# Windowed attention with a gated MLP: one free list for PSUM's eight banks, MLP sums read out by halves, a shorter weight decode, and another order of the work

## The chip, the cores and the metric

The kernel runs on one core of a Trainium2 chip. The metric is device time in microseconds (us); before the change the median of three runs is 635.64, from 635.51 to 636.7. The engines are called as the profile calls them: PE (TensorE, matmuls), PEld (its weight loads), DVE (VectorE), ACT (ScalarE), POOL (GpSimd) and SP (SyncE, which issues all DMAs).

## What is computed

Attention over a window of 128 positions with a linear bias per head, and behind it an MLP whose second half is normalised and mixed along the sequence, for 8 batches, 8 heads of 64, 576 positions:

```python
def _attn_ref(q, k, v):
    scores = scale * np.matmul(q, k.transpose(0, 1, 3, 2))
    mask = (rel >= 0) & (rel < 128)
    scores = np.where(mask, scores + bias[None], -1000000000.0)
    attn = np.exp(scores - np.max(scores, axis=-1, keepdims=True))
    attn = attn / (np.sum(attn, axis=-1, keepdims=True) + 1e-09)
    return np.matmul(attn, v)

def _moe_ref(x, w_in, g_ln, w_sg, b_sg, w_out):      # x: 8 x 576 x 512, the heads side by side
    h = gelu_tanh(x @ w_in)                          # 1024 columns
    u, v = h[..., :512], h[..., 512:]
    v_n = (v - mean(v)) / np.sqrt(var(v) + 1e-06) * g_ln
    v_s = np.einsum('ts,bsd->btd', w_sg, v_n) + b_sg[None, :, None]
    return x + (u * v_s) @ w_out
```

`w_in` and `w_out` are float64. They come to the chip as 64-bit words and are decoded there.

## The kernel before

**The attention.** The work is cut into 32 pairs: 8 batches of 4 pairs of heads. For each pair there are steps, each named by a letter and the pair's number: `q` and `L` load queries with keys, and values (SP); `a` and `c`, or `*` for both, compute the scores (PE, L247); `A`, `B`, `C`, `G` select and take row minima of the negated scores (DVE, L273 and L266); `e`, `E`, `f`, `F`, `j` are exponentials with their row sums (ACT, L282), written into a column of `stats`, ten to a pair; `R` adds 1e-9 and inverts (DVE, L294 and L295); `r`, `s`, `S` scale (POOL, L299); `t`, `T`, `z` transpose on PE (L309, L322); `X`, `Y`, `P` mask and copy the transposes (DVE L318, ACT); `2` with `v`, or `3` with `V`, are the sums with the values (PE, L329 and L342); `x` copies the result out of PSUM (ACT, L350 and L351); `h`, `l`, `k` split it into a high and a low part (ACT L356, POOL L359, ACT L362).

**The MLP.** Each product is three matmuls, high by high, high by low and low by high (`mm3`, L555 to L561). For batch b: `v{b}{t}` are the sums of the v half for row block t (in batch 0 in pieces `w{t}{c}`), `vg` their gelu out of PSUM (ACT, L633), `nv…` the steps of the norm; `tt`, `tj`, `tg`, `nt…`, `tn` do the same for the last 64 rows, the tail (tn is L595); `u{b}{f}{i}` are the sums of the u half for feature block f and half i of the 576 positions (288 columns each), `uc` copies a block's two halves into an array (ACT, L689), `ug` is the gelu over all of it; `y{b}{f}{i}` mix v along the positions, `gm` multiplies u by both halves (DVE, L712), `gh` and `gl` split the product (ACT L716, POOL L719); `Oa` and `O` are the output sums, `oa` adds x to both halves (DVE, L742) and `D` stores (SP, L754). PE takes the same number of matmuls of the same widths for all of this wherever in the program they stand.

**The weights.** Each 64-bit weight block k goes through `i` (load, SP L168), `d` (ACT, L179 and L181), `m` (DVE, L183), `b` (DVE, L185), `o` (DVE, L187), `+` (POOL, L190), `H` (ACT, L192) and `-` (L194), twelve blocks, all while the first batch is under way. The buffers `wst` that the loads fill are four, and are later used for g. The mixing weights w_sg are staged through the same buffers (`wl`, `wH`, `w-`, L522 and L523; `gb` loads g_ln).

**PSUM.** PSUM has eight banks of 512 f32 columns. Before, pool `ps_s` has two single banks, `ps_a` two single banks, and `ps_m` two tiles of two banks each. Scores and value sums use `ps_s` or `ps_a`, transposes `ps_a`, and all MLP sums `ps_m`: two row blocks of v share one tile, one bank each, and so do the two halves of a u, y or o sum.

**The order.** Nothing is reordered: the list ORDER (L780 to L841) names every step once, 1684 in all, and each engine runs its instructions in the list's order. A planner (L385 to L408) only holds that a step stands behind what it needs. So an engine whose next instruction waits holds up everything behind it; on SP that holds for a DMA that waits for a free buffer. The loop at the end of the kernel ties each instruction to the one before it on its engine.

Of the kernel before, what the change touches and what calls it, by code (L numbers as in the profile page):

```python
# [9 lines left out]
F32 = mybir.dt.float32  # L10
# [11 lines left out]
def attention_gmlp(  # L22
# [30 lines left out]
    TINY64 = 2.0 ** -15  # L53
# [16 lines left out]
    def hi_of(x):  # L70
        return x[:, 0:S]
# [99 lines left out]
    def split64(hi, lo, w, f, last):  # L171
# [9 lines left out]
        nc.scalar.activation(f, w1f, AF.Abs)  # L181
        yield
        nc.vector.tensor_scalar(f, f, TINY64, None, ALU.max)  # L183
        yield
        nc.vector.tensor_scalar(fi, fi, 3, 0x3FFFFFFF, ALU.logical_shift_left, ALU.bitwise_and)  # L185
        yield
        nc.vector.scalar_tensor_tensor(out=fi, in0=w1, scalar=-0x40000000, in1=fi, op0=ALU.bitwise_and, op1=ALU.bitwise_or)  # L187
# [20 lines left out]
    class Pair:  # L208
# [25 lines left out]
        def scores(self, *t2s):  # L234
            insts = [x for t2 in t2s for x in self.score_list(t2, ps_a if len(t2s) > 1 and t2 == 0 else ps_s)]
            burst(insts)

        def score_list(self, t2, pool):
# [5 lines left out]
            banks = self.banks[t2] = [pool.tile([P, 512], F32, name=pool.name) for _ in range(2)]  # L244
# [47 lines left out]
        def inverse(self):  # L292
            rr = self.rr = att.tile([P, NS], F32, name="rr", bufs=3)
            nc.vector.tensor_scalar(rr, self.sm, 1e-9, None, ALU.add)  # L294
            nc.vector.reciprocal(rr, rr)  # L295
# [11 lines left out]
        def transpose(self, j):  # L307
            ct = self.ct[j] = ps_a.tile([P, 512], F32, name="ps_a")
# [11 lines left out]
        def transpose_first(self):  # L320
            self.ct0 = ps_a.tile([P, 512], F32, name="ps_a")
# [5 lines left out]
        def values_first(self, pool):  # L327
            self.x2 = pool.tile([P, 512], F32, name=pool.name)
            nc.tensor.matmul(self.x2[:, 0:R], self.vd, self.p0, start=True, stop=True)  # L329
# [31 lines left out]
        def low_tail(self):  # L361
# [9 lines left out]
            "T": lambda p: p.transpose(1), "Y": lambda p: p.masked(1), "2": lambda p: p.values_first(ps_a), "v": lambda p: p.values(ps_a), "3": lambda p: p.values_first(ps_s), "V": lambda p: p.values(ps_s), "x": gather, "h": high, "l": low, "k": low_tail,  # L371
# [13 lines left out]
    class Planner:  # L385
# [23 lines left out]

    BUFS = {"ps_s": 2, "ps_a": 2, "ps_m": 2, "e": 4, "qk": 2, "vt": 2, "nb": 3, "rr": 3, "px": 2, "xf": 2 * NC, "xs": NC, "g": NF, "vg": 2, "vn": 1, "vA": 1, "u": 1, "st": 3}  # L410
# [23 lines left out]
    def add_pair(n):  # L434
# [441 lines left out]
```

## Time and profile before

| what | value |
|---|---|
| median of 3 runs | 635.64 us |
| the profiled execution's own time | 635.48 us |
| its span in the trace | 633.8 us |
| instructions in the span | 14834 |
| mean granted clock of PE | 0.985 |
| moved by DMA | 57.24 MB |

The span is what the trace covers, from the first instruction to the last; the time of the same execution is 1.7 us more. In rows of the timeline the columns are the start, the busy time of the group, engine, line, operation, what is written and read, count, and in brackets how long the engine was idle before it and what ended that. In rows that group a line, the numbers are the least, median and greatest duration in ns and the first and last start in us. A row of a stretch gives its ends and length, then the busy time of PE, PEld, DVE, ACT and POOL with the number of instructions, the granted clock of PE as a share of full speed, the busy share of the DMA engines and GB/s.

### The profile page before, as it was taken

How to read it: one execution, taken by the hardware profiler on the slowest of the kernel's cores; microseconds unless marked ns; L12 is line 12 of the kernel's file. 1: busy time of each engine (PE TensorE's matmuls, PEld its weight loads, DVE VectorE, ACT ScalarE, POOL GpSimd, SP SyncE). 2: the span in 40 equal slices, each digit the busy share in tenths (PEclk: the TensorE clock that was granted, in tenths of full speed). 3: DMA queues.
4: the chain of work that ended last, by engine and by line, in shares of the span. 5: the costliest groups of instructions: out<-in, count | busy, mean ns of one | idle time of the engine just before them, and what ended most of it. 6: DMA issues, size and time to landing. Idle time of an engine off the chain costs nothing.

```text
span 633.8 us, 14834 instructions
## 1 busy us (share of the span) xinstructions
PE 603.6 (95%) x5664; PEld 550.9 (87%) x5664; DVE 374.3 (59%) x1297; ACT 355.4 (56%) x1047; POOL 232.7 (37%) x237
## 2 busy tenths in 40 slices
PE   2687999989999999999999999999999999999997
PEld 1466799978999989998899989998999989999896
DVE  4779897537654786455723577647564565462611
ACT  6687768462673854834672578647473455543430
POOL 2668635542135222542134333542235221441220
PEclk9878999999999999999999999999999999999999
DMA  5777503241203243131220432333122311110001
GB/s 211 223 229 236 158 31 116 79 143 38 73 18 97 95 140 93 42 112 41 78 79 2 134 133 78 86 108 97 40 95 79 128 65 41 41 40 38 0 1 76
DMA packets 55931, 57.24 MB, mean 90 GB/s; under 512 B 8498, under 2 KB 45362, under 8 KB 55860
## 3 DMA queue, kind: packets, MB, share of 16 engines
q1 hardware_dynamic: 55860, 56.28, 28.5%
q8 instruction: 45, 0.74, 0.5%
q14 instruction: 26, 0.21, 0.1%
HBM read 46.83 MB, written 9.44 MB: 89 GB/s over the span
## 4 chain that ended last, share of the span: by engine, by line
PE 85%; DVE 4%; ACT 2%; issue 1%; POOL 0%; POOLq 0%; DVEq 0%
PE ps_m L559 21%; PE ps_m L561 20%; PE ps_m L560 20%; PE ps_s L342 8%; PE ps_a L309 4%; PE ps_a L247 4%; PE ps_s L247 3%; ACT e L282 1%; PE ps_m L707 1%; PE ps_m L706 1%; PE ps_m L643 1%; PE ps_m L645 1%; PE ps_s L329 1%; DVE px L318 1%; DVE e L266 1%
## 5 line engine op out<-in xcount | busy, mean ns | idle before, releaser
L282 ACT ACTIVATE e<-e,stats 128x128 f32<-128x128 f32 (+1 forms) x320 | 121.2, 381 | 39.4 <-DVE stats L266 38.4
L299 POOL TENSOR_TENSOR e<-e,rr 128x512 f32<-128x512 f32 (+1 forms) x96 | 80.1, 854 | 134.6 <-DVE rr L295 99.0
L559 PE MATMUL ps_m<-g,wo 128*128 128x288 f32 x256 | 78.7, 308 | 0.0
L559 PE MATMUL ps_m<-ws,vn 128*128 128x288 f32 x256 | 78.6, 307 | 0.0
L559 PE MATMUL ps_m<-xs,wi 128*128 128x288 f32 x256 | 77.6, 303 | 0.1
L561 PE MATMUL ps_m<-g,wo 128*128 128x288 f32 x256 | 75.8, 296 | 0.0
L561 PE MATMUL ps_m<-xs,wi 128*128 128x288 f32 x256 | 75.6, 295 | 0.0
L560 PE MATMUL ps_m<-ws,vn 128*128 128x288 f32 x256 | 75.6, 295 | 0.0
L561 PE MATMUL ps_m<-ws,vn 128*128 128x288 f32 x256 | 75.5, 295 | 0.0
L560 PE MATMUL ps_m<-xs,wi 128*128 128x288 f32 x256 | 75.5, 295 | 0.0
L560 PE MATMUL ps_m<-g,wo 128*128 128x288 f32 x256 | 74.9, 293 | 0.5 <-POOL g L719 0.5
L584 POOL TENSOR_TENSOR rs<-rs,mhalf 128x1 f32<-128x1 f32 (+1 forms) x40 | 31.4, 786 | 109.5 <-DVE rs L581 103.7
L359 POOL TENSOR_TENSOR xs<-xf,xs 128x576 fp32r<-128x576 f32 x32 | 45.4, 1425 | 62.0 <-ACT xs L356 62.0
L318 DVE TENSOR_TENSOR px<-ps_a,m_old 128x512 f32<-128x512 f32 x64 | 43.9, 686 | 41.1 <-PE ps_a L309 27.3
L719 POOL TENSOR_TENSOR g<-u,g 128x576 fp32r<-128x576 f32 x32 | 45.5, 1424 | 51.0 <-ACT g L716 51.0
L282 ACT ACTIVATION_READ_ACCUMULATOR e<-e,stats 128x1 f32 (+1 forms) x320 | 60.3, 188 | 0.0
L247 PE MATMUL ps_s<-qk 64*64 64x192 f32 (+2 forms) x632 | 42.2, 354 | 14.1 <-DMA qk<-qkT 7.9
L559 PE MATMUL ps_m<-wi,xs 128*128 128x512 f32 x128 | 53.6, 419 | 2.1 <-ACT vg L633 2.1
L712 DVE TENSOR_TENSOR u<-ps_m,u 128x576 f32<-128x576 f32 x32 | 24.1, 755 | 52.0 <-PE ps_m L707 49.8
L742 DVE TENSOR_TENSOR xf<-ps_m,xf 128x576 f32<-128x576 f32 x32 | 24.0, 752 | 49.3 <-PE ps_m L561 49.3
L560 PE MATMUL ps_m<-wi,xs 128*128 128x512 f32 x128 | 51.3, 401 | 0.0
L559 PEld LDWEIGHTS ps_m<-xs,wi 128*128 128x128 f32 x256 | 48.3, 188 | 3.4 <-issue 1.6
(122 smaller groups left out, 1523.4 us busy)
## 6 DMA issues: line engine op xcount, KB each, us to landing
qk<-qkT SPq DMA_DIRECT2D x32, 576.0 KB, 3.9
vt<-v_in SPq DMA_DIRECT2D x64, 256.0 KB, 3.5
outT<-xf SPq DMA_DIRECT2D x32, 288.0 KB, 2.1
wst<-w_in SPq DMA_DIRECT2D x8, 512.0 KB, 6.1
vt<-v_in SPq DMA_DIRECT2D x64, 32.0 KB, 3.1
wst<-w_out SPq DMA_DIRECT2D x4, 512.0 KB, 3.9
wst<-w_sgT SPq DMA_DIRECT2D x4, 288.0 KB, 5.1
vd<-v_in SPq DMA_DIRECT2D x64, 16.0 KB, 2.7
```

The source lines that it names most:

```text
L247: return lambda: nc.tensor.matmul(dst, qk[js, 0, q0:q0 + R], qk[js, 1, k0:k1], start=True, stop=True)
L282: nc.scalar.activation(x, x, AF.Exp, bias=self.nm[0:n, i:i + 1], scale=-1.0, accum_out=self.sm[0:n, i:i + 1])
L299: nc.gpsimd.tensor_tensor(x, x, self.rr[0:n, i:i + m].rearrange("p (m o) -> p m o", o=1).broadcast_to([n, m, c]), ALU.mult)
L309: burst([lambda t=t: nc.tensor.transpose(ct[:, t * P:(t + 1) * P], self.pr[j][:, t, :], ident) for t in range(T)])
L318: nc.vector.tensor_tensor(xv[:, :, :, i, :], cv, m.rearrange("p (t h c) -> p t h c", t=1, h=1).broadcast_to([P, T, 2, R]), ALU.mult)
L342: return lambda: nc.tensor.matmul(x1[heads[j], q0 + lo // 2 * R if t < 0 else q0 + t * R:q0 + (hi + 1) // 2 * R], block, px[j][:, (half * ...
L359: nc.gpsimd.tensor_tensor(lo_of(self.xs), self.xf, hi_of(self.xs).bitcast(F32), ALU.subtract)
L559: nc.tensor.matmul(dst, ah, bh, start=(first and i == 0), stop=False)
L560: nc.tensor.matmul(dst, ah, bl, start=False, stop=False)
L561: nc.tensor.matmul(dst, al, bh, start=False, stop=(last and i == n - 1))
L584: nc.gpsimd.tensor_tensor(x["rs"][0:rows], x["rs"][0:rows], mhalf[0:rows], ALU.pow)
L719: nc.gpsimd.tensor_tensor(st[f"g{f}"][:, 1, :], st["u"][:, f, :], st[f"g{f}"][:, 0, :].bitcast(F32), ALU.subtract)
```

## The change

Five edits.

1. **Decode.** Step `m`, the maximum with TINY64, is gone for all twelve blocks. ACT's Abs (L181) multiplies by a constant REBASE, the shift has no mask behind it, and the combine takes only the sign bit.
2. **PSUM.** The three pools become eight fixed one-bank tiles. The planner hands them out while it goes through the order: a step gets the bank that has been free longest, and a bank is free again when the last step that reads it stands in the order ahead of the new one. Any step can get any bank.
3. **Halves.** Each v, u, y and o sum has a bank of its own, and what reads a sum reads one half: two copies `uc`, two multiplications `gm` and two additions `oa` of 288 columns each in place of one of 576. `Oa` and `O` are split the same way; `D` waits for both halves.
4. **Eleven columns.** `stats` and `rr` have one column more, so that L294 and L295 run over eleven columns in place of ten.
5. **The order.** ORDER is a new list, of 1808 steps.

```diff
-    TINY64 = 2.0 ** -15
+    REBASE = 2.0 ** (-(1023 - 127) // 8)
...
-    ps_s = ctx.enter_context(tc.tile_pool(name="ps_s", bufs=2, space=PSUM))
-    ps_a = ctx.enter_context(tc.tile_pool(name="ps_a", bufs=2, space=PSUM))
-    ps_m = ctx.enter_context(tc.tile_pool(name="ps_m", bufs=2, space=PSUM))
+    ps = ctx.enter_context(tc.tile_pool(name="ps", bufs=1, space=PSUM))
+    NB = 8
+    psum = [ps.tile([P, 512], F32, name=f"bank{i}") for i in range(NB)]
+    given = []
+
+    def bank():
+        return psum[given.pop(0)]
...
-        x = const.tile([P, 2, NS], F32, name=f"stats{i}")
+        x = const.tile([P, 2, NS + 1], F32, name=f"stats{i}")
...
-        nc.scalar.activation(f, w1f, AF.Abs)
+        nc.scalar.activation(f, w1f, AF.Abs, scale=REBASE)
         yield
-        nc.vector.tensor_scalar(f, f, TINY64, None, ALU.max)
+        nc.vector.tensor_scalar(fi, fi, 3, None, ALU.logical_shift_left)
         yield
-        nc.vector.tensor_scalar(fi, fi, 3, 0x3FFFFFFF, ALU.logical_shift_left, ALU.bitwise_and)
-        yield
-        nc.vector.scalar_tensor_tensor(out=fi, in0=w1, scalar=-0x40000000, in1=fi, op0=ALU.bitwise_and, op1=ALU.bitwise_or)
+        nc.vector.scalar_tensor_tensor(out=fi, in0=w1, scalar=-0x80000000, in1=fi, op0=ALU.bitwise_and, op1=ALU.bitwise_or)
...
-            rr = self.rr = att.tile([P, NS], F32, name="rr", bufs=3)
+            rr = self.rr = att.tile([P, NS + 1], F32, name="rr", bufs=3)
...
+            at = {n: i for i, n in enumerate(order)}
+            free = [-1] * NB
             for n in order:
                 _, _, _, run, after, _, take, _, _ = self.steps[n]
                 assert done.issuperset(after), n
                 for c, users in take:
+                    if c == "ps":
+
+                        i = free.index(min(free))
+                        assert free[i] < at[n], n
+                        free[i] = max(at[u] for u in users)
+                        given.append(i)
+                        continue
...
             def run():
-                key = f"pv{t // 2 * 2}"
+                key = f"pv{t}"
                 if key not in st:
-                    st[key] = ps_m.tile([P, 2, 512], F32, name="ps_m")
+                    st[key] = bank()
...
-            def gate():
-                u = st["u"][:, f, :]
-                nc.vector.tensor_tensor(in2(u), st[f"py{f}"][:, :, 0:S2], in2(u), ALU.mult)
+            def gate(i):
+                def run():
+                    u = st["u"][:, f, halves[i]]
+                    nc.vector.tensor_tensor(u, st[f"py{f}{i}"][:, 0:S2], u, ALU.mult)
+                return run
...
-        y731 Oa7 gm73 gh73 gl73 O70 O72 oa70 D70 O73 oa72 D72 O71 oa73 D73 oa71 D71
+        gl71 gl70 gl72 Oa71 Oa70 gm730 oa631 D63 gh73 gl73 O700 O701 oa700 oa701 O730 oa730 oa600 O731 oa731 O720 O721 oa720
+        oa721 D72 D62 D73 D60 D70 D61 O710 O711 oa710 oa711 D71
```

Three places where the order moves instructions. In the changed kernel line numbers differ a little: L168 has become L172, L185 L187, L187 L189, L273 L275, L266 L268, and `mm3`'s L559 to L561 are L569 to L571.

The first is the start of SP's list, which issues all loads. `wst` are the decode buffers (weights), `qk` queries with keys of one pair, `vt` and `vd` the values of one pair. Before:

```order
L168 DMA wst<-w_in 128x512
L221 DMA qk<-qkT 128x1152
L168 DMA wst<-w_sgT 128x576
L221 DMA qk<-qkT 128x1152
L168 DMA wst<-w_in 128x512 x2
L168 DMA wst<-w_sgT 128x576 x2
L550 DMA gb<-g_ln 128x512
L221 DMA qk<-qkT 128x1152
L168 DMA wst<-w_in 128x512
L229 DMA vt<-v_in 128x4x128
```

The changed kernel's start of the same list:

```order
L223 DMA qk<-qkT 128x1152
L172 DMA wst<-w_in 128x512 x3
L223 DMA qk<-qkT 128x1152
L172 DMA wst<-w_in 128x512
L223 DMA qk<-qkT 128x1152
L231 DMA vt<-v_in 128x4x128
L232 DMA vt<-v_in 64x128
L231 DMA vt<-v_in 128x4x128
```

Pair 0's queries have become the first load; its values stand behind four weight blocks, the number of the buffers, and the mixing weights behind those values.

The second place is DVE's start: the decode of the first two or three weight blocks (`tmp`) among pair 0's minima (the select into PSUM; each is followed by its minima, left out here). Before, it goes on from the second half of pair 0's first scores:

```order
L183 TENSOR_SCALAR tmp<-tmp 128x512 x2
L185 TENSOR_SCALAR tmp<-tmp 128x512
L187 SCALAR_TENSOR_TENSOR tmp<-wst,tmp 128x512
L185 TENSOR_SCALAR tmp<-tmp 128x512
L273 COPY_PREDICATED ps_s<-sel,ps_s 128x2x64
```

The changed kernel, from the same half on:

```order
L275 COPY_PREDICATED bank_68<-sel,bank_68 128x2x64
...
L187 TENSOR_SCALAR tmp<-tmp 128x512
L189 SCALAR_TENSOR_TENSOR tmp<-wst,tmp 128x512
L275 COPY_PREDICATED bank_69<-sel,bank_69 128x2x64
...
L275 COPY_PREDICATED bank_70<-sel,bank_70 128x2x64
```

Before, five decode steps of two weight blocks stand between the two halves of the minima of pair 0. In the changed kernel the shift of the second block and the first block's combine are left there, and the shift of a third block comes behind pair 0's last minima.

The third place is PE at the first two v sums of batch 1, v10 and v11 (`xs` the split attention result, `wi` the weights, `g` and `wo` those of the output sums). Before, the end of v10 and the start of v11:

```order
L561 MATMUL ps_m_1777<-wi_141,xs_1612 128x512
L559 MATMUL ps_m_1777<-wi_141,xs_1658 128x512 [waits Activation_49]
L560 MATMUL ps_m_1777<-wi_141,xs_1658 128x512
L561 MATMUL ps_m_1777<-wi_141,xs_1658 128x512 [waits Pool_49]
L559 MATMUL ps_m_1777<-wi_141,xs_1649 128x512 [waits Activation_49]
L560 MATMUL ps_m_1777<-wi_141,xs_1649 128x512
```

The changed kernel, the end of v11 and the start of v10:

```order
L571 MATMUL bank1_68<-wi_143,xs_1604 128x512 [waits Pool_49]
L569 MATMUL bank5_72<-g_1377,wo_144 128x288 [waits DVE_49]
...
L570 MATMUL bank5_72<-g_1379,wo_144 128x288
L571 MATMUL bank5_72<-g_1379,wo_144 128x288
L569 MATMUL bank6_73<-wi_143,xs_1527 128x512 [waits DVE_49]
```

Both sums had the same tile, and the second waited for ACT at its first matmul; now they have two banks with twelve matmuls of an output sum between them, and the second waits for a DVE step there.

More of the change, by code (lines that the diff above doesn't have):

```diff
@@ L234, in scores, with score_list @@
         def scores(self, *t2s):
-            insts = [x for t2 in t2s for x in self.score_list(t2, ps_a if len(t2s) > 1 and t2 == 0 else ps_s)]
+            insts = [x for t2 in t2s for x in self.score_list(t2)]
             burst(insts)
-        def score_list(self, t2, pool):
+        def score_list(self, t2):
             qk, heads = self.qk, self.heads
@@ L243, in score_list @@
                 self.e0 = e0s[self.n % 2]
-            banks = self.banks[t2] = [pool.tile([P, 512], F32, name=pool.name) for _ in range(2)]
+            banks = self.banks[t2] = [bank() for _ in range(2)]
             def score(dst, js, q0, k0, k1):
@@ L307, in transpose @@
         def transpose(self, j):
-            ct = self.ct[j] = ps_a.tile([P, 512], F32, name="ps_a")
+            ct = self.ct[j] = bank()
             burst([lambda t=t: nc.tensor.transpose(ct[:, t * P:(t + 1) * P], self.pr[j][:, t, :], ident) for t in range(T)])
@@ L320, in transpose_first @@
         def transpose_first(self):
-            self.ct0 = ps_a.tile([P, 512], F32, name="ps_a")
+            self.ct0 = bank()
             nc.tensor.transpose(self.ct0[:, 0:P], self.e0, ident)
@@ L452, in add_pair @@
         else:
-            put("*", "PE", 1.9, [f"q{n}", ("z", n - 2)], take=es + [("ps_a", [f"A{n}"]), ("ps_a", [f"B{n}"]), ("ps_s", [f"C{n}"]), ("ps_s", [f"G{n}"])])
+            put("*", "PE", 1.9, [f"q{n}", ("z", n - 2)], take=es + [("ps", [f"A{n}"]), ("ps", [f"B{n}"]), ("ps", [f"C{n}"]), ("ps", [f"G{n}"])])
             put("A", "DVE", 0.9, [f"*{n}", ("R", n - 3)])
@@ L654, in his @@
                 return [st["vA"][0:R], vB[0:R]]
-            add(f"tt{b}", "PE", 1.9, at, sums, [f"k{n}" for n in mine] + rows + [f"{k}{c}" for c in range(NC) for k in "-H"], take=[("ps_m", [f"tj{b}"])])
+            add(f"tt{b}", "PE", 1.9, at, sums, [f"k{n}" for n in mine] + rows + [f"{k}{c}" for c in range(NC) for k in "-H"], take=[("ps", [f"tj{b}"])])
             add(f"tj{b}", "DVE", 1.35, at - AHEAD, join, [f"tt{b}"], take=[("vg", [f"tn{b}"]), ("vg", [f"tj{b}"])])
@@ L722, in add_y @@
                 need = [f"tn{b}", f"nt{b}h"] + [f"vn{b}{t}" for t in range(T)] + (["t-", "b-", "tH"] + [f"w-{c}" for c in range(T)] if b == 0 else [])
-                add(f"y{b}{f}{i}", "PE", 1.87, at + 1.87 * STRETCH * i, sums(i), need + ([f"y{b}{f}0"] if i else []), take=[] if i else [("ps_m", [f"gm{b}{f}"])])
-            add(f"gm{b}{f}", "DVE", 0.69, at - AHEAD, gate, [f"y{b}{f}1", f"ug{b}"])
-            add(f"gh{b}{f}", "ACT", 0.6, at - AHEAD, high, [f"gm{b}{f}"] + (["bH", "tl"] + [f"i{8 + c}" for c in range(NF)] if b == 0 else []), take=[("g", [f"O{b}{c}" for c in range(NC)])])
+                add(f"y{b}{f}{i}", "PE", 1.87, at + 1.87 * STRETCH * i, sums(i), need, take=[("ps", [f"gm{b}{f}{i}"])])
+                add(f"gm{b}{f}{i}", "DVE", 0.37, at - AHEAD, gate(i), [f"y{b}{f}{i}", f"ug{b}"])
+            add(f"gh{b}{f}", "ACT", 0.6, at - AHEAD, high, [f"gm{b}{f}0", f"gm{b}{f}1"] + (["bH", "tl"] + [f"i{8 + c}" for c in range(NF)] if b == 0 else []), take=[("g", [f"O{b}{c}{i}" for c in range(NC) for i in range(2)])])
             add(f"gl{b}{f}", "POOL", 1.39, at - AHEAD, low, [f"gh{b}{f}"])
```

240 lines of the change are left out of this document (125 added, 115 removed).

## The prediction

> **What bounds the kernel now.** I read the page first: the busy line, then the slices, which say where PE is not full.
>
> ```profile
> PE 603.6 (95%) x5664; PEld 550.9 (87%) x5664; DVE 374.3 (59%) x1297; ACT 355.4 (56%) x1047; POOL 232.7 (37%) x237
> PE   2687999989999999999999999999999999999997
> ```
>
> PE is the bound over most of the span, and only slices 0 to 3, 8 and the last show it short. So I cut the span at those places and asked for the busy time of each engine there.
>
> ```profile
> core 0: us, PE busy (x) PEld busy (x) DVE busy (x) ACT busy (x) POOL busy (x), PEclk, DMA share, GB/s
> 0.00:7.40 7.40, 0.09 (x4) 0.09 (x7) 1.85 (x14) 6.19 (x18) 1.93 (x14) 1.00 0.56 190
> 7.40:26.60 19.20, 11.39 (x113) 7.83 (x113) 14.07 (x64) 11.21 (x41) 10.77 (x9) 1.00 0.63 207
> 26.60:39.80 13.20, 9.51 (x89) 7.61 (x89) 7.57 (x35) 9.71 (x38) 6.97 (x7) 0.61 0.95 284
> 39.80:65.30 25.50, 21.44 (x238) 16.45 (x239) 24.07 (x100) 19.96 (x72) 19.15 (x17) 0.93 0.71 222
> 65.30:95.20 29.90, 29.48 (x272) 25.91 (x272) 26.04 (x52) 22.07 (x51) 14.80 (x15) 1.00 0.28 83
> ...
> 95.80:137.90 42.10, 42.10 (x436) 39.65 (x434) 25.34 (x120) 26.57 (x100) 20.33 (x18) 1.00 0.36 109
> 137.90:146.00 8.10, 5.98 (x21) 4.63 (x21) 2.52 (x7) 2.86 (x5) 3.39 (x4) 0.79 0.33 109
> 146.00:610.00 464.00, 463.69 (x4355) 429.51 (x4355) 267.75 (x904) 254.50 (x723) 150.94 (x151) 1.00 0.23 72
> 610.00:633.80 23.80, 19.32 (x144) 18.86 (x143) 4.55 (x6) 1.79 (x3) 4.42 (x4) 0.96 0.13 50
> ```
>
> Three stretches differ in what limits them. The opening, up to 95.8, leaves PE idle for some 23 us; its DVE is busy 24.07 of 25.50 and 26.04 of 29.90 us in the two later stretches. From 95.8 on PE has no gap but the one at 137.9. The end, from 610, is a chain. In the middle VectorE has 196 us of room, so whatever the change does to VectorE and ScalarE there is covered.
>
> The opening ends where the first y sum starts, since PE runs without a gap from there to 137.9. The timeline around it and the two lines of the decode that the edit touches:
>
> ```profile
> 94.41 0.75 DVE L595 SCALAR_TENSOR_TENSOR vA<-vg,rs,vA 64x512 fp32r<-64x512 f32 x1
> 95.77 0.40 PE L559 MATMUL ps_m<-ws,vn 128*128 128x288 f32 x1
> L183 DVE TENSOR_SCALAR tmp<-tmp x12: 409/422/520, 7.4 to 91.1; 128x512 f32<-128x512 f32 x12
> L185 DVE TENSOR_SCALAR tmp<-tmp x12: 366/420/429, 7.9 to 94.0; 128x512 int32<-128x512 int32 x12
> ```
>
> The last step of the tail's norm, tn0 (L595), ends at 95.16; the y sum needs it, and PE had only the scores of a new pair to run meanwhile. Ahead of tn0 both lists give VectorE the same steps, but for the twelve maxima and the shifts b8 and b9, which now come behind it. PE also has nearly the same steps ahead of that sum. So the opening's length is VectorE's work ahead of tn0 plus VectorE's waits.
>
> **The opening: −9.0.** Work removed: 12 × 0.42 = 5.1 for the maxima and 2 × 0.42 = 0.8 for the two shifts, 5.9 in all. ACT's Abs keeps its instruction with another scale, and shift and combine keep theirs with other constants: nothing. VectorE's waits from 7.4 to 95.2 are, by the rows above, 5.1 + 5.6 + 1.4 + 3.9 = 16.0. What makes the early ones:
>
> ```profile
> 10.48 7.61 SPq L168 DMA_DIRECT2D wst<-w_sgT  x2
> 14.43 0.76 DVE L183 TENSOR_SCALAR tmp<-tmp 128x512 f32<-128x512 f32 x2 [3.46 <-ACT tmp L181]
> 17.44 2.52 PE L247 MATMUL ps_s<-qk 64*64 64x64 f32 x24 [4.78 <-issue]
> 19.86 0.42 SPq L229 DMA_DIRECT2D vt<-v_in  x1
> 29.31 0.66 PE L329 MATMUL ps_a<-p,vd 128*128 128x64 f32 x2 [2.78 <-DMA vd<-v_in]
> 29.90 3.47 PE L342 MATMUL ps_a<-px,vt 128*64 128x64 f32 x36
> 39.98 1.88 PE L342 MATMUL ps_a<-px,vt 128*64 128x64 f32 x36
> ```
>
> SP stands 7.6 us at weight loads that wait for a decode buffer, and the first values are issued behind them, at 19.86; PE then waits 2.78 us for them. VectorE stands 3.46 us at two maxima whose weights are not there, with the rest of pair 0's row minima queued behind them, and PE's next scores 4.78 us behind those. The new rows on SP put pair 0's values ninth in the list, with no load ahead of them that waits for a decode buffer. VectorE's leave one shift of the second weight block ahead of the rest of pair 0's minima, and that block's load is third on SP where it was fifth. That can take away the 3.46 of VectorE's wait and the 2.78 of PE's. Against it stands how full the other engines become: PE's 72.5 us of the opening (sum of the rows) start at 7.3, so an opening of 83.8 (12 less) would leave PE 4.0 idle, and ACT's 69.7 us only 14.1. Three engines that feed each other were never that full together before 65.3. So I take half of those two waits, 3.1, and the sum is −5.9 − 3.1 = −9.0. The ends: all of the waits before 39.8 (10.7) gone too, −16.6; or only the instructions gone, −5.9.
>
> Eleven columns in place of ten, in the add of 1e-9:
>
> ```profile
> L294 DVE TENSOR_SCALAR rr<-stats x32: 157/173/1191, 19.3 to 562.1; 128x10 f32<-128x10 f32 x32
> ```
>
> Thirty-two short instructions, one of 1191 ns at 59.2 against a median of 173. If the odd count freed it of that wait, it would be −1.0 in the opening; one column more is otherwise nothing. I take 0 and keep −1.0 as the end. The Trainium skill, "VectorE: DVE Perf Modes", section "What auto-detection actually checks", speaks against a gain: two SBUF ports are used when the outermost counts of source and destination are both even or equal, and eleven equals eleven; by it the term is 0.
>
> **The stall at 137.9: −3.8.**
>
> ```profile
> 137.49 0.40 PE L560 MATMUL ps_m<-wi,xs 128*128 128x512 f32 x1
> 137.73 0.39 PE L561 MATMUL ps_m<-wi,xs 128*128 128x512 f32 x1
> 140.24 0.58 PE L559 MATMUL ps_m<-wi,xs 128*128 128x512 f32 x1 [2.12 <-ACT vg L633]
> 144.45 0.39 PE L561 MATMUL ps_m<-wi,xs 128*128 128x512 f32 x1
> 138.30 1.28 ACT L633 ACT_TABLE_LOAD   x1
> ```
>
> v11 writes the other half of the tile that gelu vg10 reads, and so waits for ACT, which loads a table first. From 137.73 to 144.45 are twelve matmuls at 6.72 us, where 0.24 each would make 2.9: 3.8 lost, 2.1 in the wait and 1.7 at the lower clock behind it (0.79 in the row above). With a bank of its own for each v sum nothing reads v10's partner any more, and the new order puts output sums between. The Trainium skill, "TensorE: Matmul & The Clock Gate", Part 1, says the clock falls after a window of some 3.4 us without work; by it the stall would cost 2.1 alone and the term be −2.1, but here 2.1 us of waiting were followed by eleven matmuls at 0.38.
>
> **Block entries: −1.2.** An MLP sum behind pair work begins more slowly:
>
> ```profile
> 571.99 0.40 PE L559 MATMUL ps_m<-g,wo 128*128 128x288 f32 x1
> 572.23 0.30 PE L560 MATMUL ps_m<-g,wo 128*128 128x288 f32 x1
> 572.37 0.29 PE L561 MATMUL ps_m<-g,wo 128*128 128x288 f32 x1
> ```
>
> The first step is 0.24, the next 0.14: 0.10 for each entry. Behind the first y sum, PE's rows in order enter an MLP sum from pair work 98 times before and 74 now: −2.4. Pair steps that now follow each other may pay something alike that no row here shows; I take half, and keep 0 and −2.4.
>
> **Reading out by halves: 0.**
>
> ```profile
> L712 DVE TENSOR_TENSOR u<-ps_m,u 128x576 f32<-128x576 f32 x32 | 24.1, 755 | 52.0 <-PE ps_m L707 49.8
> L689 ACT COPY u<-ps_m x32: 613/640/649, 80.2 to 601.5; 128x576 f32<-128x576 f32 x32
> ```
>
> Thirty-two more gates and thirty-two more last adds (the same shape). A half takes at least half of 0.755, so nothing more in sum, and at most the whole, 64 × 0.755 = 48 us of VectorE; the 32 copies at most 20 of ACT. VectorE's 196 us of room and ACT's 210 hide even the upper ends, so the term is 0; without that cover it would lie between nothing and 48. PE's matmuls are the same in number and width.
>
> **The end: +0.2.**
>
> ```profile
> 619.41 0.40 PE L560 MATMUL ps_m<-g,wo 128*128 128x288 f32 x1 [0.54 <-POOL g L719]
> 629.90 0.76 DVE L742 TENSOR_TENSOR xf<-ps_m,xf 128x576 f32<-128x576 f32 x1 [2.41 <-PE ps_m L561]
> 631.50:632.00 0.50, 0.00 (x0) 0.00 (x0) 0.00 (x0) 0.00 (x0) 0.00 (x0) 1.00 0.98 392
> ```
>
> Half a gate in the chain to the wait at 619.41 and half a last add at 629.90: −0.35 each, though of the first wait at most 0.54 is there. But SP's last stores are now D72 D62 D73 D60 D70 D61 D71, and D72 waits for the sums of the next-to-last output block, some 3 us before PE ends. Seven outputs of 288 KB at 392 GB/s are 5.2 us, against about 3 before the last one may start and 0.74 for itself: up to +0.9 more. Ends −0.7 and +0.9.
>
> **New waits: +1.8.** The new list lets the v sums of batches 1 to 7 stand 3.2 to 3.9 us of PE work behind the last values of their batch, six times of seven (3.2 to 11.5 before). The chain to be hidden:
>
> ```profile
> 199.08 0.59 ACT L350 COPY xf<-ps_s 128x512 f32<-128x512 f32 x1 [3.74 <-PE ps_s L342]
> 200.56 1.43 POOL L359 TENSOR_TENSOR xs<-xf,xs 128x576 fp32r<-128x576 f32 x1 [2.34 <-ACT xs L356]
> ```
>
> From 199.08 to 201.99 are 2.9 us where ACT and POOL are free, and the first nine of a v sum's twelve matmuls need only earlier pairs (another 2.1). It fits; between none late (0) and one stall like 137.9 (+3.8) I take the middle.
>
> **Sum.** −9.0 − 3.8 − 1.2 + 0.2 + 1.8 = −12.0 from the profiled execution's 635.48 (span 633.8 and 1.7 around it; 0.16 under the median of the runs): **623.5 us**. Its own ends: 617.4 with the other half of the two waits gone, −2.4 at the entries and no new waits; 630.5 with −5.9 in the opening, 0 at the entries, +0.9 at the end, +3.8 in new waits.
>
> **The rivals.** B: the opening loses every wait before 39.8: −16.6, so 635.48 − 16.6 − 3.8 − 1.2 + 0.2 + 1.8 = 615.9, at best 612.9 (entries −2.4, no new waits). For it: SP's row order removes just these causes. Against: PE would have to be full from 7.3 on, and more than that unless the 0.61 clock of 26.6 to 39.8 goes too (v0 took 3.47, the next values 1.88).
>
> C: PE, not VectorE, bounds the opening. Its first stretches go to the low clock whenever it waits, as v0 did, and what VectorE saves comes back as such matmuls. Opening 0: 632.5. Against: PE's sums there waited for VectorE and DMA, not the reverse.
>
> D, slower: the split chain of a batch's last pair comes late by over 2.1 + 0.4 us because ACT and POOL have other steps queued ahead of it; then v sums stop, and each stop costs as much as at 137.9, 3.8. Six batches: 22.8 in place of 1.8, so 644.5. It is slower than before from four such stops on (15.2 against 13.8 gained without the new waits). For it: the distance shrank in most batches. Against: VectorE, ACT and POOL have room there.
>
> E, the change doesn't do what it says: the removed 5.9 us turn into waits for weights (DMA 0.95 busy in 26.6 to 39.8) and ACT, entries give nothing, and new waits and end take their upper bound: −3.8 + 3.8 + 0.9 = +0.9, 636.4, no change.
>
> **Chances.** Forecast 0.70, B 0.13, C 0.06, D 0.06, E 0.05. A measurement of this kernel can tell about 0.2% (1.3 us) from no change. Faster: 0.70 + 0.13 + 0.06 = 0.89; same 0.05; slower 0.06. The range of 613 to 631 holds the forecast's ends and B, and leaves out C, D and E, 0.17.
>
> **What would show it.** Right: the first y sum at about 87 us, no VectorE wait of 3 us before 20, pair 0's values without the DMA wait; no gap at the second v sum of batch 1 and a granted clock of 1.0 there; the stretch from the first y sum to the last one some 5 us shorter less any new gap; the last store's data still queued when PE ends. Wrong: a first y sum at 90 us or later (only the instructions went, or C), new PE gaps at v or u sums with ACT or POOL named as releaser (D), or a gap that stays at the first gelu of a batch.

## The result

The changed kernel takes 617.81 us (median of 4 runs, 617.0 to 618.0), the kernel before 636.07 (4 runs beside them, 635.51 to 636.7). The ratio is 0.971, with a 95% interval of 0.9693 to 0.9727: faster by 18 us, where 12 were forecast (623.5, range 613 to 631). The profiled execution took 618.0 us, with a span of 616.3 in place of 633.8.

The page's first lines after the change, to be held against those of before:

```profile
span 616.3 us, 14851 instructions
PE 591.5 (96%) x5664; PEld 548.5 (89%) x5664; DVE 375.5 (61%) x1349; ACT 358.8 (58%) x1083; POOL 230.2 (37%) x237
```

PE takes the same 5664 matmuls in 12 us less busy time. The share of busy time hides where that lies, so I cut the span at the first and the last y sum again. First the two ends of the middle in the changed kernel, then the last y sum of before:

```profile
85.87 0.40 PE L569 MATMUL bank<-ws,vn 128*128 128x288 f32 x1
...
597.89 0.30 PE L718 MATMUL bank<-wsB,vB 66*128 66x288 f32 x1
```

```profile
616.05 0.30 PE L707 MATMUL ps_m<-wsB,vB 66*128 66x288 f32 x1
```

| stretch | before | after | measured | forecast |
|---|---|---|---|---|
| opening, to the first y sum | 95.77 | 85.87 | −9.9 | −9.0 |
| middle, first to last y sum | 520.28 | 512.02 | −8.3 | −3.8 − 1.2 + 1.8 = −3.2 |
| from there to the end of the span | 17.7 | 18.4 | +0.7 | +0.2 |

So the opening and the end came near to their terms, and nearly all of the 6 us that the forecast lacked lie in the middle.

**The opening after.** The stretches of the changed kernel, with columns as before:

```profile
7.40:26.60 19.20, 8.99 (x101) 6.27 (x95) 15.26 (x60) 13.94 (x52) 10.21 (x9) 1.00 0.82 275
26.60:39.80 13.20, 10.49 (x120) 9.13 (x122) 11.08 (x57) 10.98 (x41) 8.87 (x10) 0.76 0.93 321
39.80:65.30 25.50, 24.05 (x241) 19.04 (x238) 20.91 (x80) 23.22 (x79) 20.25 (x18) 0.99 0.54 164
```

```profile
0.00:85.90 85.90, 66.80 (x715) 56.18 (x715) 68.33 (x248) 67.01 (x218) 53.12 (x61) 0.96 0.62 201
```

VectorE's busy time ahead of the first y sum is 68.3 where it was 74.2 (the rows of before added up), 5.9 less; its idle time is 17.6 where it was 21.6, 4.0 less. The terms were 5.9 and 3.1. Busy time here includes time in which an instruction stands blocked: one shift takes 3.17 us where 0.43 is the median (more on it below), and in the kernel before one combine took 2.28 and one subtraction 1.96, where 0.69 and 0.72 are the medians. These about cancel. From 39.8 on PE is now nearly full (24.05 of 25.50, then without a pause), so that VectorE alone no longer sets the pace there.

**The end after.** SP's last stores, then the row of the stretch in which they land:

```profile
608.83 3.81 SPq L770 DMA_DIRECT2D outT<-xf  x7
```

```profile
611.50:612.50 1.00, 0.00 (x0) 0.00 (x0) 0.45 (x1) 0.00 (x0) 0.00 (x0) 1.00 1.06 415
612.50:613.50 1.00, 0.00 (x0) 0.00 (x0) 0.00 (x0) 0.00 (x0) 0.00 (x0) 1.00 1.05 408
613.50:614.50 1.00, 0.00 (x0) 0.00 (x0) 0.00 (x0) 0.00 (x0) 0.00 (x0) 0.60 1.04 410
```

Seven stores are issued in 3.8 us, and the DMA engines are full for three microseconds behind PE's end, as the prediction said. PE's last matmul starts at 611.16 and takes 0.29; from its end to the span's are 4.8 us, 3.9 before.

### The profile page after: what moved, and what is told of

Same layout as the page of the kernel before. It is cut to its first block, busy times and chain, and to the rows that moved or that the text cites. A ratio compares the mean times of both kernels' runs of the same rounds, so it can differ in the third digit from the quotient of the medians.

```text
span 616.3 us, 14851 instructions
## 1 busy us (share of the span) xinstructions
PE 591.5 (96%) x5664; PEld 548.5 (89%) x5664; DVE 375.5 (61%) x1349; ACT 358.8 (58%) x1083; POOL 230.2 (37%) x237
## 4 chain that ended last, share of the span: by engine, by line
PE 83%; ACT 5%; DVE 4%; POOL 3%; DMA 2%; issue 2%; SPq 0%; POOLq 0%; ACTq 0%; DVEq 0%
PE bank L569 20%; PE bank L570 19%; PE bank L571 19%; PE bank L344 9%; PE bank L249 6%; PE bank L311 4%; ACT e L284 2%; DMA wst<-w_in 1%; PE bank L718 1%; PE bank L717 1%; PE bank L653 1%; PE bank L655 1%; DVE e L268 1%; DVE px L320 1%; POOL e L301 1%
## 5 line engine op out<-in xcount | busy, mean ns | idle before, releaser
L569 PE MATMUL bank<-g,wo 128*128 128x288 f32 x256 | 78.1, 305 | 0.0
L569 PE MATMUL bank<-ws,vn 128*128 128x288 f32 x256 | 77.8, 304 | 0.0
L569 PE MATMUL bank<-xs,wi 128*128 128x288 f32 x256 | 77.3, 302 | 0.0
L570 PE MATMUL bank<-g,wo 128*128 128x288 f32 x256 | 75.7, 296 | 0.3 <-POOL g L732 0.3
L571 PE MATMUL bank<-g,wo 128*128 128x288 f32 x256 | 75.6, 295 | 0.0
L571 PE MATMUL bank<-xs,wi 128*128 128x288 f32 x256 | 75.6, 295 | 0.0
L570 PE MATMUL bank<-xs,wi 128*128 128x288 f32 x256 | 75.6, 295 | 0.0
L570 PE MATMUL bank<-ws,vn 128*128 128x288 f32 x256 | 75.6, 295 | 0.0
L571 PE MATMUL bank<-ws,vn 128*128 128x288 f32 x256 | 75.4, 295 | 0.0
L249 PE MATMUL bank<-qk 64*64 64x192 f32 (+2 forms) x1280 | 56.7, 318 | 11.6 <-DMA qk<-qkT 11.0
L344 PE MATMUL bank<-px,vt 128*64 128x128 f32 (+1 forms) x1152 | 63.3, 266 | 1.9 <-DVE px L320 1.9
L344 PEld LDWEIGHTS bank<-px,vt 128*64 128x64 f32 x1152 | 58.7, 142 | 7.0 <-issue 2.9
L320 DVE TENSOR_TENSOR px<-bank,m_old 128x512 f32<-128x512 f32 x64 | 43.8, 684 | 28.0 <-PE bank L311 16.9
L268 DVE CUSTOM_DVE_ANT_0 e<-bank,bias 128x128 f32<-128x128 f32 (+1 forms) x256 | 59.2, 269 | 2.2
L249 PEld LDWEIGHTS bank<-qk 64*64 64x64 f32 x1280 | 44.1, 140 | 17.0 <-DMA qk<-qkT 11.6
L724 DVE TENSOR_TENSOR u<-bank,u 128x288 f32<-128x288 f32 x64 | 27.5, 451 | 45.7 <-PE bank L718 32.3
```

The source lines that it names most:

```text
L249: return lambda: nc.tensor.matmul(dst, qk[js, 0, q0:q0 + R], qk[js, 1, k0:k1], start=True, stop=True)
L268: nc.vector.tensor_tensor_reduce(out=dst, in0=src, in1=bs, scale=-1.0 / math.sqrt(D), scalar=3e38, op0=ALU.add, op1=ALU.min, accum_out=acc)
L320: nc.vector.tensor_tensor(xv[:, :, :, i, :], cv, m.rearrange("p (t h c) -> p t h c", t=1, h=1).broadcast_to([P, T, 2, R]), ALU.mult)
L344: return lambda: nc.tensor.matmul(x1[heads[j], q0 + lo // 2 * R if t < 0 else q0 + t * R:q0 + (hi + 1) // 2 * R], block, px[j][:, (half * ...
L569: nc.tensor.matmul(dst, ah, bh, start=(first and i == 0), stop=False)
L570: nc.tensor.matmul(dst, ah, bl, start=False, stop=False)
```

## The experiments

Times are given as ratios to the kernel before on the same chip; the changed kernel, run again beside the last three, stood at 0.9701 (0.9676 to 0.9727). A difference of 0.001 is 0.64 us. Most of the runs' intervals are 0.004 to 0.005 wide, so that where a microsecond matters the profile's stretches decide: the middle of the changed kernel came out at 512.00 to 512.06 in all seven profiles in which it was left as it is. The openings differ more from execution to execution: in these kernels the first y sum stands between 82.1 and 86.7 (89.9 with the maxima), and in two traces with the order of before it stands at 95.77 and at 94.31 (before_gelu_late, which is the same up to there).

### The maxima alone: max_back and before_no_max

The first puts a maximum with 0 back ahead of each shift of the changed kernel; the second takes the maxima out of the kernel before, with the new decode's constants, and leaves its order and pools.

```diff
         nc.scalar.activation(f, w1f, AF.Abs, scale=REBASE)
         yield
+        nc.vector.tensor_scalar(f, f, 0.0, None, ALU.max)
+        yield
         nc.vector.tensor_scalar(fi, fi, 3, None, ALU.logical_shift_left)
```

> The changed kernel with a VectorE maximum put back into each of the twelve weight decodes, right ahead of the shift (a maximum with 0 of an absolute value, so it changes no number). Theory 1, the opening lasts as long as VectorE's work ahead of the tail's norm: the first y sum comes 12 x 0.42 = 5.1 us later, the whole is 4 to 6 us longer (about 623). Rival 2, the new opening is bounded by PE and ScalarE (PE is busy 24.05 of 25.50 us from 39.8 to 65.3 and 29.90 of 29.90 behind it), and the order made the gain: the maxima fit into VectorE's waits, 0 to 2 us longer.

> The kernel before with the new decode alone: no maximum, its order of the remaining steps, its pools and its sums untouched. Theory 1: the first y sum comes 5 us sooner and the whole is 5 us shorter (about 631). Rival 2, the opening of before waits for loads and ScalarE at the places where the maxima stood, so that their time comes back as waits: 0 to 2 us shorter. Whatever is missing up to the 9.9 us that the opening gained is the order's.

Measured: with the maxima back 0.9823 (0.9801 to 0.9844), without them in the old order 0.9961 (0.9944 to 0.9977). The first y sums in the two profiles, max_back first:

```profile
89.91 0.40 PE L572 MATMUL bank<-ws,vn 128*128 128x288 f32 x1
```

```profile
92.83 0.40 PE L556 MATMUL ps_m<-ws,vn 128*128 128x288 f32 x1
```

Put back, the maxima cost 4.0 us up to the first y sum (89.91 against 85.87) and 4.7 over the span; by the ratios it is more, 5 to 11 us with both intervals taken in. In the new order only ten of the twelve stand ahead of the tail's norm, and 10 × 0.42 makes 4.2; the other two are in the middle, which is 0.7 longer (512.73). Taken out of the old order they are worth 2.9 us of profile (92.83 against 95.77; against the other trace's 94.31 it would be 1.5) and 1.5 to 3.6 of run. The stretch up to the first y sum and the shifts, in the kernel before without the maxima and then in the one before (behind the second bar stand the idle time and what ended it):

```profile
0.00:92.80 92.80, 69.10 (x714) 55.42 (x714) 71.86 (x252) 69.51 (x219) 53.60 (x62) 0.98 0.59 186
```

```profile
L183 DVE TENSOR_SCALAR tmp<-tmp 128x512 int32<-128x512 int32 x12 | 6.4, 544 | 7.7 <-ACT tmp L181 7.6
```

```profile
0.00:95.80 95.80, 72.51 (x715) 58.20 (x715) 74.19 (x263) 69.72 (x219) 53.62 (x61) 0.93 0.58 180
```

```profile
L185 DVE TENSOR_SCALAR tmp<-tmp 128x512 int32<-128x512 int32 x12 | 4.9, 418 | 0.2
```

VectorE's busy time falls by 2.3 and not by 5.1: the twelve shifts now take 6.4 where they took 4.9, two instructions of the next pair's minima (0.3 each) now fall into the stretch, and the wait for ACT's decode, which ended at the maxima, ends at the shifts. So theory 1 holds in its kind, since VectorE's work counts in both orders, but the old order gives back only a good half of the price. The other 7 of the 9.9 us need the new order, the banks, or both. That they can do without the removed work is seen in max_back, whose VectorE is as busy as before (74.1) and whose first y sum still comes 5.9 sooner:

```profile
0.00:89.90 89.90, 68.01 (x714) 57.45 (x714) 74.10 (x257) 67.51 (x218) 53.19 (x61) 0.87 0.61 192
```

The new order with the old pools was not tried, so order and banks are not told apart.

### The gelu behind the second sum: before_gelu_late

```diff
-        ... O01 v10 vg10 oa01 v11 s9 vg11 ...
+        ... O01 v10 oa01 v11 vg10 s9 vg11 ...
```

> The kernel before with one step moved: the gelu of batch 1's first v sum stands behind the second v sum instead of ahead of it, so that PE's second sum no longer waits for it in the tile that they share. Theory: the 2.1 us wait at 137.9 and the matmuls at low clock behind it go, 3 to 4 us shorter (about 632). Rival: the wait moves on to the next sum that needs that tile, and less than 1 us is gained.

Measured: 0.9935 (0.9915 to 0.9955), 4.1 us. The stretch with the two sums, where PE had been busy 5.98 of 8.10 us at a clock of 0.79:

```profile
135.00:144.50 9.50, 9.50 (x52) 8.04 (x51) 5.25 (x13) 4.21 (x14) 5.58 (x7) 1.00 0.29 96
```

PE is busy throughout at full clock, and the middle of this kernel is 516.39, 3.9 less than before. The stall's term of 3.8 is right, and it needs no change of PSUM: one step's place in the list does it. The prediction's "eleven matmuls at 0.38" is a mean, though: behind the wait nine start 0.38 to 0.43 us apart, and then they are back at 0.23. In the kernel before the granted clock there is 0.50:

```profile
140.50:143.90 3.40, 3.40 (x9) 2.63 (x9) 0.75 (x3) 0.00 (x0) 1.79 (x2) 0.50 0.72 230
```

### Values and scores next to each other: sum_inside_values and sum_behind_sums

The first adds a matmul to the values step, the second the same to output sums:

```diff
-            burst([part(half, t, j) for half, t in order for j in (1, 0)])
+            insts = [part(half, t, j) for half, t in order for j in (1, 0)]
+            if self.n >= 6:
+                insts.insert(18, lambda: nc.tensor.matmul(self.x2[:, 64:288], wi[:, 0, 0, 0:P], ws[:, 0, 0, 0:224], start=True, stop=True, skip_group_check=True))
+            burst(insts)
```

> The changed kernel with one matmul added (128 x 128 by 128 x 224 of weights, into columns that nobody reads) in the middle of the 36 matmuls of the values of pairs 6 to 31: 26 times from half-width matmuls to a full one and back. Compared with the next kernel, which has the same 26 matmuls without such a turn. Theory, by the gaps between starts in the profile (a full matmul ahead of half-width ones 0.09 longer, the first one behind them 0.105 longer, the last half-width one 0.10 longer): 0.3 each, 7 to 8 us longer than the next kernel. The prediction's price of 0.10 for each: 2.6. Rival, such turns cost nothing: 0.

> The changed kernel with the same 26 matmuls added behind output sums of batches 0 to 6, where full matmuls stand anyway. Every theory: 26 times about 0.11, 2.8 us longer than the changed kernel.

Measured: 0.9797 (0.9777 to 0.9816) and 0.9735 (0.9714 to 0.9756); the middles are 516.93 and 514.74, against 512.02. The second is as expected (2.72 for 26). The first, 2.19 above it by the middles (3.9 by the ratios, 1.3 to 6.5 with both intervals), fell short of my theory's 7 to 8, for a reason in the kernel: in PE's row order the added matmul stands behind the 36, not among them, so it is a turn of its own only where the values were followed by a score or a transpose and not by an MLP sum. By the trace that is 14 of the 26 places: 10 ahead of scores, 4 ahead of transposes. The 2.19 us of difference are then 0.2 for each of the ten, and little for the others:

```profile
324.48 0.37 PE L349 MATMUL bank<-ws,wi 128*128 128x224 f32 x1
324.79 1.65 PE L249 MATMUL bank<-qk 64*64 64x64 f32 x40
```

At all ten places the added matmul takes 0.300 to 0.304 up to the first score; behind output sums it takes 0.100 to 0.107. That is the price of the very thing that the new list changes, and it can be read off the other rows too. Before, a pair's scores stand between MLP sums:

```profile
393.92 0.30 PE L707 MATMUL ps_m<-wsB,vB 66*128 66x288 f32 x1
394.14 0.94 PE L247 MATMUL ps_a<-qk 64*64 64x64 f32 x22
...
395.73 0.40 PE L559 MATMUL ps_m<-ws,vn 128*128 128x288 f32 x1
395.96 0.29 PE L560 MATMUL ps_m<-ws,vn 128*128 128x288 f32 x1
```

After, they stand behind another pair's values:

```profile
403.47 1.88 PE L344 MATMUL bank<-px,vt 128*64 128x64 f32 x36
405.27 1.65 PE L249 MATMUL bank<-qk 64*64 64x64 f32 x40
406.86 0.40 PE L569 MATMUL bank<-g,wo 128*128 128x288 f32 x1
407.09 0.30 PE L570 MATMUL bank<-g,wo 128*128 128x288 f32 x1
```

The forty score matmuls take 1.59 in both (394.14 to 395.73, 405.27 to 406.86), and the first sum behind them 0.23 where 0.13 is the rule. But before, the last sum ahead of the scores also takes 0.22; after, the values' 1.80 up to the scores is what they take anywhere. A stretch of values or scores among full matmuls thus costs 0.09 on leaving the sums and 0.10 on coming back, and two such stretches side by side pay that once. A stretch of transposes costs nothing:

```profile
405.94 0.30 PE L707 MATMUL ps_m<-wsB,vB 66*128 66x288 f32 x1
406.07 0.60 PE L309 MATMUL ps_a<-ident,e 128*128 128x128 f32 x4
406.43 0.38 PE L559 MATMUL ps_m<-ws,vn 128*128 128x288 f32 x1
406.65 0.29 PE L560 MATMUL ps_m<-ws,vn 128*128 128x288 f32 x1
```

(From 406.07 to 406.65 are 0.58 for four transposes at 0.109 and a sum at 0.133, which make 0.57.) In the middle, by PE's starts, the sums are left for scores 4 times where it was 25 times, and come back from scores or values 24 times where it was 43: 21 × 0.09 + 19 × 0.10 = 3.8. With transposes and the values' 128 × 128 matmuls counted among the full ones, PE goes over to the smaller matmuls of scores and values 30 times where it was 51, and as often back.

### Gates in two steps: gates_in_two_steps

```diff
                     u = st["u"][:, f, halves[i]]
-                    nc.vector.tensor_tensor(u, st[f"py{f}{i}"][:, 0:S2], u, ALU.mult)
+                    y = st[f"py{f}{i}"][:, 0:S2]
+                    nc.vector.tensor_tensor(y, y, u, ALU.mult)
+                    nc.vector.tensor_copy(u, y)
```

> The changed kernel with each of the 64 gates as two VectorE instructions of the same width (the product back into its bank, and a copy from there) in place of one: some 64 x 0.45 = 29 us more of VectorE. By the prediction VectorE's room in the middle hides it: 0 to 1 us longer, of which up to 0.5 at the end, where the last gate is in the chain. Rival, the list leaves no room at these places: 5 us or more.

Measured: 0.9779 (0.975 to 0.9807), 5 us longer than the changed kernel. Its middle is 517.14, 5.1 longer, with 28.6 us more of VectorE:

```profile
PE 593.2 (95%) x5664; PEld 548.1 (88%) x5664; DVE 404.1 (65%) x1413; ACT 359.4 (58%) x1083; POOL 230.1 (37%) x237
```

So the rival's 5 us came. In the middle PE's waits for POOL, VectorE and ACT are 3.5 us in this kernel, 0.6 in the changed one. Held start against start with the changed kernel, whose matmuls in the middle are the same, nearly all of the 5.1 us arises at nine places, eight of them with such a wait: the matmuls next to a wait start later than its idle time alone would make them. What the change itself adds is far smaller:

```profile
L724 DVE TENSOR_TENSOR u<-bank,u x64: 395/456/458, 90.5 to 598.2; 128x288 f32<-128x288 f32 x64
L755 DVE TENSOR_TENSOR xf<-bank,xf x64: 395/453/458, 116.2 to 611.5; 128x288 f32<-128x288 f32 x64
```

A half takes 0.456 where the whole took 0.755, so halving adds 64 × 0.456 − 32 × 0.755 = 5 us for the gates and as much for the last adds. That was hidden, as far as the middle shows; 28.6 us more were not, so the room of 196 us would hardly have hidden 48.

### The opening's loads and one shift: values_behind_weights and shift_later

The first moves the load of pair 0's values on SP behind the two weight blocks that wait for a buffer, the second moves one block's decode on VectorE:

```diff
-        ... c1 i6 q2 L0 wl2 wl0 q3 C1 ...
+        ... c1 i6 q2 wl2 wl0 q3 L0 C1 ...
```

```diff
-        ... wH0 b6 o6 w-2 +4 +6 w-0 a2 X0 Y0 A2 ...
+        ... wH0 w-2 +4 w-0 a2 X0 Y0 b6 o6 +6 A2 ...
```

> The changed kernel with pair 0's values loaded behind the two blocks of mixing weights, which wait for a decode buffer, and the fourth queries: SP's order at this place as it was before the change. By the prediction's half of two waits (3.1 us in all, 2.78 of it PE's wait for these values): PE waits for the values again, 1.5 to 3 us longer. Rival: by the time the values come, VectorE's masks are what PE waits for, so 0 to 0.5.

> The changed kernel with the decode of the fourth loaded block (shift, combine, and POOL's addition behind it) moved behind pair 0's masked multiplications on VectorE. In the changed kernel's profile that shift took 3165 ns at 20.34 (median 426) while POOL ran three instructions without a gap, and pair 0's masks stood behind it until 24.14. Theory: the masks start 3 us sooner, the shift meets a pause of POOL, and the first y sum comes 2 to 4 us sooner (about 614.5). Rival: the opening is bounded elsewhere behind it, or the shift is blocked as long at its new place: 0 to 1 us.

Measured: 0.9728 (0.9706 to 0.975) for the values, against 0.9701: 1.7 us longer with intervals that overlap. Its trace shows the old wait again, and its first y sum comes at 86.67, against 85.20 in the trace of the changed kernel run beside it and 85.87 in the first. Here the wait and the values' sums behind it, and below the same sums in the changed kernel:

```profile
25.84 0.41 PE L331 MATMUL bank<-p,vd 128*128 128x64 f32 x2 [1.96 <-DMA vd<-v_in]
26.17 3.70 PE L344 MATMUL bank<-px,vt 128*64 128x64 f32 x36
```

```profile
26.08 0.34 PE L344 MATMUL bank<-px,vt 128*64 128x64 f32 x4 [1.66 <-DVE px L320]
```

So the rival is what these two traces show. In the changed kernel PE stands at the same place for VectorE's masks, and the sums start at 26.08 instead of 26.17. From 40 to 82 us PE's starts in the two traces differ by 0.02; the 0.8 between the first y sums arises at 82, behind a later weight load for which ACT waits 2.28 us in place of 1.45, and whether that comes from the moved loads was not followed. The trace run beside it is ahead by 1.0 already at 17, before the moved loads matter. What the order of the loads is worth where VectorE's masks come sooner, as in the next kernel, stays open.

The shift: 0.9689 (0.9667 to 0.9711), 1 us less than the changed kernel, within the intervals. What it was about is seen in the changed kernel's timeline at 20:

```profile
20.34 3.17 DVE L187 TENSOR_SCALAR tmp<-tmp 128x512 int32<-128x512 int32 x1
20.57 1.40 POOL L533 TENSOR_TENSOR ws<-wst,ws 128x576 fp32r<-128x576 f32 x1
...
21.93 1.28 POOL L192 TENSOR_TENSOR tmp<-tmp,wst 128x512 int32<-128x512 int32 x1
...
24.14 0.68 DVE L320 TENSOR_TENSOR px<-bank,m_old 128x512 f32<-128x512 f32 x1
```

and with the shift moved:

```profile
20.45 0.69 DVE L320 TENSOR_TENSOR px<-bank,m_old 128x512 f32<-128x512 f32 x1 [0.39 <-PE bank L311]
...
21.57 1.28 POOL L192 TENSOR_TENSOR tmp<-tmp,wst 128x512 int32<-128x512 int32 x1
21.65 0.68 DVE L320 TENSOR_TENSOR px<-bank,m_old 128x512 f32<-128x512 f32 x1
...
22.84 0.42 DVE L187 TENSOR_SCALAR tmp<-tmp 128x512 int32<-128x512 int32 x1
```

The masks read PSUM and run beside POOL; the shift, from and to SBUF, takes 3.17 us until POOL pauses at 23.21, and 0.42 when POOL is idle. The first y sum comes at 83.35, 2.5 sooner than in the changed kernel's first profile. The median gains less, probably because the long shift comes only in some executions: of the seven profiles with the shift at its old place and the loads as changed, apart from max_back, three (both of the changed kernel and gates_in_two_steps) have it above 3.1 us and a first y sum at 85.2 to 85.9; the others have it at 0.55 us and, but for one at 84.96, a first y sum at 82.1 to 83.2. The Trainium skill, "SBUF — State Buffer", section "Who interferes with whom", has the rule: VectorE in a two-port mode and GpSimd exclude each other for whole instructions, whoever starts first. The rows agree as to the blocking (no row shows a mode), and add that here POOL's next two instructions, which followed without a pause, went ahead of the waiting one.

### Ten columns: ten_columns

```diff
-        x = const.tile([P, 2, NS + 1], F32, name=f"stats{i}")
+        x = const.tile([P, 2, NS], F32, name=f"stats{i}")
...
-            rr = self.rr = att.tile([P, NS + 1], F32, name="rr", bufs=3)
+            rr = self.rr = att.tile([P, NS], F32, name="rr", bufs=3)
```

> The changed kernel with ten columns in the row sums and their inverses again. By the prediction's term of 0: same within 0.5 us, with the longest of the 32 adds again near 1 us, as with eleven columns (1009 ns). If eleven columns spared a wait, it is 1 us or more longer, and an add stands far above 1009 ns.

Measured: 0.9705 (0.968 to 0.973), no difference that the runs can tell. The adds with ten columns and, below, with eleven in the changed kernel:

```profile
L296 DVE TENSOR_SCALAR rr<-stats x32: 154/173/1005, 16.3 to 529.4; 128x10 f32<-128x10 f32 x32
```

```profile
L296 DVE TENSOR_SCALAR rr<-stats x32: 154/173/1009, 17.4 to 533.1; 128x11 f32<-128x11 f32 x32
```

The two are alike to a few ns, the longest included. The eleventh column spares no wait here.

### The last stores, and both moves together: stores_sooner, shift_and_stores

```diff
-        ... oa721 D72 D62 D73 D60 D70 D61 O710 O711 oa710 oa711 D71
+        ... oa610 D61 ... oa620 D62 ... oa701 D70 ... oa600 D60 ... oa731 D73 ... oa721 D72 O710 O711 oa710 oa711 D71
```

> The changed kernel with the last stores of batches 6 and 7 each issued right behind the addition that completes it, instead of six of them behind the last addition but two halves. Theory: the data of the last store no longer queues behind six others; from PE's last matmul to the end come 3.9 us as before the change instead of 4.8, 0.9 us shorter (about 617). Rival: the last store's time is its own, no difference within 0.3.

> The changed kernel as it is, for the three kernels beside it on the same chip: 617 to 618 where its opening goes as in its profile, 614 to 615 where the shift that stood 3165 ns finds a pause of POOL.

> The changed kernel with both moves: the fourth loaded block's shift behind pair 0's masks, and each last store right behind the addition that completes it. If both effects stand and add: 2 to 3 us from the shift where it was blocked, 0.9 to 1.2 from the stores, about 613.5 to 614.

Measured: 0.9709 (0.9695 to 0.9722) for the stores, which no run can tell from the changed kernel. Their trace shows the last store issued 0.82 behind the start of PE's last matmul (1.12 in the kernel before, where the addition is a whole one), and the span of 614.2 ending 3.6 us behind PE, not 4.8:

```profile
610.26 0.29 PE L571 MATMUL bank<-g,wo 128*128 128x288 f32 x1
610.59 0.46 DVE L755 TENSOR_TENSOR xf<-bank,xf 128x288 f32<-128x288 f32 x1 [1.13 <-PE bank L571]
611.08 0.33 SPq L770 DMA_DIRECT2D outT<-xf  x1
```

The changed kernel run again: 616.85 us, from 614.62 to 617.63. Both moves together: 614.02 us (5 runs, 613.8 to 615.54), 0.9667 (0.9645 to 0.969). By its ratio that is the fastest kernel measured: clearly faster than the one before, and 2.8 us under the changed one by the medians, though the two intervals just overlap.

## Why the prediction came out as it did

**The opening, −9.0 forecast, −9.9 measured: right in size, in part by luck.** VectorE's busy time fell by the 5.9 us that were counted, and its waits fell by 4.0 where 3.1 were taken. But the 5.9 and the rest do not simply add: in the old order the maxima were worth only 2.9. The waits that went are not those that the prediction halved. VectorE's 3.46 us ahead of 20 are still there, as 3.64 (first row below), against the prediction's own sign; PE's 2.78 for pair 0's values have become 1.66 for VectorE's masks; what VectorE no longer waits for stands mostly behind 28, such as 2.54 us for a transpose at 35.27. (In SP's list the values are eighth, not ninth.) And the profile that gave −9.9 is one in which a shift stood blocked for 2.7 us; four traces without that have the first y sum at 82.1 to 85.0, 10.8 to 13.7 sooner than 95.77. The argument that the opening is VectorE's work plus its waits holds as an account; as a forecast it needs the order that turns the work into time. Rival B (every wait before 39.8 gone) was too hopeful: VectorE still stands 3.6 us for the first decode, and PE 6.2 for the second pair's queries, though with the shift not blocked its 16.6 is missed by 3 to 6 us only. Rival C fell: PE is nearly full from 39.8 on, and still the opening is 9.9 shorter.

```profile
11.25 0.43 DVE L187 TENSOR_SCALAR tmp<-tmp 128x512 int32<-128x512 int32 x1 [3.64 <-ACT tmp L185]
...
14.01 3.04 PE L249 MATMUL bank<-qk 64*64 64x64 f32 x40 [6.23 <-DMA qk<-qkT]
```

**The stall, −3.8 forecast, −3.9 shown** by moving one step, clock and all.

**Block entries, −1.2 forecast, −3.8 by rows and counts: the term that was mis-sized.** The step that failed is "I take half": the 98 and 74 entries are right (50 and 45 of them stand behind transposes, which cost nothing), and 0.10 for each return from scores or values stands in the runs, but the prediction had a row for the way back alone. Leaving the sums for scores costs another 0.09, and the pair steps that now follow each other pay nothing alike. The bound of −2.4 was therefore no bound. Of the middle's 8.3 us the stall is 3.9, these turns 3.8; some 0.5 is left, which single gaps can hold and no experiment settles.

**New waits, +1.8 forecast: hardly any came.** From the first to the last y sum PE's one new wait of note is for POOL, at 97:

```profile
97.59 0.66 PE L311 MATMUL bank<-ident,e 128*128 128x128 f32 x4 [0.56 <-POOL e L301]
```

No v sum waits, so the chain of 2.9 us behind a batch's last values fits into the 3.2 to 3.9, as the prediction worked out; the middle between 0 and 3.8 was caution without a row. Rival D fell with it.

**Halves, 0 forecast: right in the result, wrong in its reason.** What is left of the middle has no room for a price of the halves, though no kernel was run without them. But the 196 us of VectorE's room are an average; 28.6 us put into one kind of step cost 5.

**Eleven columns, 0: shown by the adds. The end, +0.2 forecast, +0.7 measured:** the queue behind the last store made 0.9 (4.8 against 3.9 behind PE's end), which the prediction had as its upper bound; its own figures, 5.2 − 3 − 0.74, make 1.5. Taking the queue away again gave 1.2 in the trace.

## What to carry to other kernels

Count what it costs PE to go from full matmuls to smaller tiles and back on both sides, and put the small ones next to each other; here that was as much as a stall that anyone sees in the timeline. An instruction removed from the engine that bounds a stretch was worth its whole time only in the new order (4.0 of 4.2 us), not in the old one (2.9 of 5.1). And idle time of an engine is not cover: what counts is whether it is free where the step is in a chain.

## What the runs showed of the hardware that I had not expected

- A VectorE shift of 512 columns from SBUF to SBUF took 3165 ns in place of 426, while POOL ran two instructions of 1.40 and 1.28 us without a pause after the one that was running when it began. In traces of kernels with the same order at this place the shift is blocked in three and takes 0.55 us in four.
- From start to start, a matmul of 288 columns takes 0.22 ahead of 64 × 64 score matmuls and 0.23 behind them, 0.13 among its like; around 128 × 128 transposes nothing is lost.
- After 2.12 us without work PE's next nine matmuls started 0.38 to 0.43 us apart in place of 0.24, at a granted clock of 0.50; without that wait the 3.9 us come back whole.
